# An attention and SwiGLU kernel: the halves of the attention weights on ScalarE and GpSimd, a plan entry for them, and a third factor from hi and u

## The chip, the cores and the metric

One core of one Trainium2 chip. The metric is the device time of one execution in microseconds (us); executions of one kernel agree within about 0.2%, so differences of 1 to 2 us are near the limit of what medians tell, and smaller ones are read from traces.

## The reference, cut to what matters

```python
def mab(q, kv):                       # attention with scale 1/sqrt(C)
    s = scale * (q @ kv.transpose(0, 2, 1))
    a = np.exp(s - s.max(-1, keepdims=True)); a /= a.sum(-1, keepdims=True) + 1e-09
    return a @ kv
h = mab(I, x)                         # 4 batches, 12416 tokens, 32 inducing points, C = 128
x2 = mab(x, h)
xn = x2 / rms(x2) * rms_g             # SwiGLU feed-forward, hidden width 1536
out = (silu(xn @ w_gate) * (xn @ w_val)) @ w_out
```

The kernel folds h into the gate and value weights, so that the feed-forward reads the attention weights themselves (32 per token) and not x2.

## The kernel before

The tokens go through in 100 units of mostly 512; each unit has 12 steps, one for 128 hidden channels: 1200 steps. A step is a gate matmul, silu on ScalarE, an output product of an older step, a value matmul, and u = silu x value on VectorE.

```python
ps_gv = pool("ps_gv", 4, space=PSUM)          # banks of gate and value
...
for j in range(NJ):
    g = ps_gv.tile(...);  nc.tensor.matmul(g[:, 0:T], sg[:, ts(j, P)], a[:, 0:T], start=True, stop=True)
    nc.scalar.activation(sl[:, 0:T], g[:, 0:T], AF.Silu)
    products(j)                               # output products of older steps
    v = ps_gv.tile(...);  nc.tensor.matmul(v[:, 0:T], sv[:, ts(j, P)], a[:, 0:T], start=True, stop=True)
    nc.vector.tensor_tensor(out=t[:, 0:T], in0=sl[:, 0:T], in1=v[:, 0:T], op=ALU.mult)
    steps(j)                                  # pieces of attention work, splits among them
    if (b, u, j) in ready:
        soon(1, lambda j=j, t=t: three(j, t)) # u as three factors, one step later
    else:
        plain.append(lambda j=j, t=t: project(wo[:, j, :], t[:, 0:T]))
```

A plain output product is a full fp32 matmul. In some steps u is written as hi + lo, and three single-pass matmuls, with hi, lo and a third factor d, take its place. ScalarE makes hi and a scaled hi (hs), GpSimd makes lo and d:

```python
def three(j, t):
    ...
    nc.scalar.activation(hi, v, AF.Copy, scale=1.0 - 2.0 ** -13)
    nc.gpsimd.tensor_tensor(out=lo, in0=v, in1=hi.bitcast(F32), op=ALU.subtract)
    def rest():                               # one step later
        nc.scalar.activation(hs[:, 0:T], hi.bitcast(F32), AF.Copy, scale=2.0 ** -12)
        nc.gpsimd.tensor_tensor(out=d, in0=hs[:, 0:T], in1=lo.bitcast(F32), op=ALU.subtract)
```

Every four units the attention weights of the next four are turned and split into halves of their own, also called hi and lo. This is the "split" of the text; 28 of them, nearly all at step 9 of a unit:

```python
def split():
    nc.vector.transpose(out=aT[rows, 0:w], in_=sc[b][rows, cols2[s]])
    nc.vector.tensor_copy(out=hi[rows, 0:w], in_=aT[rows, 0:w])
    nc.vector.tensor_tensor(out=lo[rows, 0:w], in0=aT[rows, 0:w], in1=hi[rows, 0:w].bitcast(F32), op=ALU.subtract)
```

Which steps get three factors is planned when the program is built. seam_busy says for how many us a piece of attention work keeps ScalarE and GpSimd busy; a step whose three factors would come too late by this count stays plain.

## Time and profile before

| | before |
|---|---|
| time, median of 4 (range) | 1717.5 us (1717.0 to 1718.2) |
| TensorE / VectorE / ScalarE / GpSimd busy | 98 / 69 / 71 / 69% |
| three-factor products of 1200 | 401 |
| lo of the split on VectorE, 28 of them: shortest / median / longest | 0.41 / 1.60 / 1.67 us |

### The profile page before, as it was taken

To read this page: it belongs to the slowest core of one execution; us is meant where nothing else is said; L and a number is where in the kernel's file an instruction comes from. 1 tells how busy PE (TensorE), PEld (TensorE's weight loads), DVE (VectorE), ACT (ScalarE), POOL (GpSimd) and SP (SyncE) were. 2 spreads that over 40 slices of the span, in tenths; PEclk is the share of its full clock that TensorE was granted. 3 is DMA by queue.
4 is the path that set the end of the run, shared out by engine and by line. 5 is a ranking of instruction groups with operands and counts; after the bars stand their busy time and mean duration, and the time that the engine had idled before them with its cause. 6 is when DMAs were issued, how large, how long until landed. Compare 5 with 4: busy or idle time off the path is not lost. (4 is left out here: it accounts for less than half of the span.)

```text
span 1715.7 us, 23430 instructions
## 1 busy us (share of the span) xinstructions
PE 1675.3 (98%) x6855; PEld 1046.2 (61%) x6855; DVE 1189.4 (69%) x1982; ACT 1222.4 (71%) x2180; POOL 1181.4 (69%) x936
## 2 busy tenths in 40 slices
PE   9899999999999999999999999999999999999998
PEld 7545565655566656665556656566556666666666
DVE  4867876777668776667667877667767666666665
ACT  4346777676777777776777777767677887788786
POOL 0317775776487776676657877577657888888875
PEclk9999999999999999999999999999999999999999
DMA  6344433433343232434334314153211121112111
GB/s 248 87 68 74 81 69 78 103 80 64 62 79 63 47 71 41 105 76 91 67 59 83 58 34 83 36 129 77 50 30 35 32 38 31 35 34 37 31 36 24
DMA packets 389359, 112.65 MB, mean 66 GB/s; under 512 B 365136, under 2 KB 369776, under 8 KB 386672
## 3 DMA queue, kind: packets, MB, share of 16 engines
q1 hardware_dynamic: 388944, 111.02, 32.3%
q8 instruction: 54, 0.88, 0.2%
q14 instruction: 73, 0.60, 0.1%
q10 hardware_dynamic: 288, 0.15, 0.0%
HBM read 53.95 MB, written 27.00 MB: 47 GB/s over the span
## 5 line engine op out<-in xcount | busy, mean ns | idle before, releaser
L607 DVE TENSOR_TENSOR u<-silu,gv 128x512 f32<-128x512 f32 (+2 forms) x1200 | 788.2, 665 | 471.9 <-PE gv L605 276.6
L602 ACT ACTIVATE silu<-gv 128x512 f32<-128x512 f32 (+2 forms) x1200 | 698.6, 584 | 414.7 <-PE gv L600 377.2
L550 PE MATMUL acc<-u,wo 128*128 128x512 f32 (+2 forms) x1598 | 793.9, 581 | 7.0 <-DVE u L607 5.8
L605 PE MATMUL gv<-a,sv 128*128 128x512 f32 (+2 forms) x1200 | 768.1, 640 | 1.3 <-ACT silu L602 0.7
L588 POOL TENSOR_TENSOR xn<-u,xn 128x512 fp32r<-128x512 f32 (+2 forms) x401 | 507.8, 1266 | 314.7 <-ACT xn L587 250.0
L593 POOL TENSOR_TENSOR xn<-hs,xn 128x512 fp32r<-128x512 f32 (+2 forms) x401 | 507.0, 1264 | 53.4 <-POOL xn L588 16.7
L600 PE MATMUL gv<-a,sg 128*128 128x512 f32 (+2 forms) x1200 | 492.5, 410 | 14.3 <-ACT silu L602 6.5
L600 PEld LDWEIGHTS gv<-a,sg 128*128 128x128 f32 x1200 | 227.6, 190 | 255.3 <-ACT silu L602 117.1
L550 PEld LDWEIGHTS acc<-u,wo 128*128 128x128 f32 x1598 | 299.1, 189 | 87.5 <-issue 17.9
L605 PEld LDWEIGHTS gv<-a,sv 128*128 128x128 f32 x1200 | 227.7, 190 | 196.5 <-issue 142.3
L587 ACT ACTIVATE xn<-u 128x512 fp32r<-128x512 f32 (+2 forms) x401 | 248.1, 619 | 18.8 <-DVE u L607 18.1
L592 ACT ACTIVATE hs<-xn 128x512 f32<-128x512 f32 (+2 forms) x401 | 246.3, 614 | 8.8 <-POOL xn L593 8.2
L550 PE MATMUL acc<-xn,xn 128*128 128x512 f32 (+2 forms) x401 | 159.0, 396 | 6.2 <-POOL xn L593 5.9
L568 PE MATMUL u<-xn,xn 128*128 128x512 f32 (+2 forms) x401 | 155.8, 388 | 0.0
L566 PE MATMUL u<-xn,xn 128*128 128x512 f32 (+2 forms) x401 | 155.4, 388 | 0.0
L492 POOL TENSOR_TENSOR rs<-ms,mhalf 128x16 f32<-128x16 f32 (+2 forms) x28 | 75.5, 2698 | 43.0 <-DVE ms L490 42.9
L550 PEld LDWEIGHTS acc<-xn,xn 128*128 128x128 f32 x401 | 75.3, 188 | 29.9 <-POOL xn L593 14.1
L568 PEld LDWEIGHTS u<-xn,xn 128*128 128x128 f32 x401 | 75.4, 188 | 17.1
L566 PEld LDWEIGHTS u<-xn,xn 128*128 128x128 f32 x401 | 75.3, 188 | 15.6
L559 DVE STREAM_TRANSPOSE o<-o 128x512 f32<-128x512 f32 (+2 forms) x97 | 67.7, 698 | 3.4
L558 DVE TENSOR_TENSOR o<-acc,o 128x512 f32<-128x512 f32 (+2 forms) x97 | 64.9, 669 | 0.0
L571 ACT ACTIVATE o<-u 128x512 f32<-128x512 f32 (+2 forms) x97 | 56.4, 582 | 0.2
(155 smaller groups left out, 746.2 us busy)
## 6 DMA issues: line engine op xcount, KB each, us to landing
out_dram<-o SPq DMA_DIRECT2D x320, 64.0 KB, 2.0
xT<-in_x_dram SPq DMA_DIRECT2D x60, 256.0 KB, 4.6
xn<-in_x_dram SPq DMA_DIRECT2D x60, 256.0 KB, 4.4
a<-hi SPq DMA_DIRECT2D x160, 64.0 KB, 2.0
a<-lo SPq DMA_DIRECT2D x158, 64.0 KB, 2.0
w<-w SPq DMA_DIRECT2D x22, 256.0 KB, 3.2
xn<-in_x_dram SPq DMA_DIRECT2D x5, 1024.0 KB, 10.8
out_dram<-o SPq DMA_DIRECT2D x64, 60.0 KB, 2.0
```

What stands on the lines that cost most here:

```text
L492: nc.gpsimd.tensor_tensor(out=rs, in0=ms, in1=mhalf[rows, 0:n], op=ALU.pow)
L550: nc.tensor.matmul(acc[:, 0:T], lhsT, rhs, start=st["left"] == NJ, stop=st["left"] == 1)
L566: nc.tensor.matmul(ups[:, 0:T], w[:, i, :], hi, start=st["k"] == nk, stop=False)
L568: nc.tensor.matmul(ups[:, 0:T], w[:, NK + i, :], lo, start=False, stop=not st["k"])
L587: nc.scalar.activation(hi, v, AF.Copy, scale=1.0 - 2.0 ** -13)
L588: nc.gpsimd.tensor_tensor(out=lo, in0=v, in1=hi.bitcast(F32), op=ALU.subtract)
L592: nc.scalar.activation(hs[:, 0:T], hi.bitcast(F32), AF.Copy, scale=2.0 ** -12)
L593: nc.gpsimd.tensor_tensor(out=d, in0=hs[:, 0:T], in1=lo.bitcast(F32), op=ALU.subtract)
L600: nc.tensor.matmul(g[:, 0:T], sg[:, ts(j, P)], a[:, 0:T], start=True, stop=True)
L602: nc.scalar.activation(sl[:, 0:T], g[:, 0:T], AF.Silu)
L605: nc.tensor.matmul(v[:, 0:T], sv[:, ts(j, P)], a[:, 0:T], start=True, stop=True)
L607: nc.vector.tensor_tensor(out=t[:, 0:T], in0=sl[:, 0:T], in1=v[:, 0:T], op=ALU.mult)
```

## The change

Its intent is to free VectorE at the splits, by giving hi to ScalarE and lo to GpSimd, to tell the plan so, and to make d without lo: hi(1 + 2^-12) - u is the same number as hi x 2^-12 - (u - hi).

```diff
-            nc.vector.tensor_copy(out=hi[rows, 0:w], in_=aT[rows, 0:w])
-            nc.vector.tensor_tensor(out=lo[rows, 0:w], in0=aT[rows, 0:w], in1=hi[rows, 0:w].bitcast(F32), op=ALU.subtract)
+            if b or s:
+                nc.scalar.copy(out=hi[rows, 0:w], in_=aT[rows, 0:w])
+            else:
+                nc.vector.tensor_copy(out=hi[rows, 0:w], in_=aT[rows, 0:w])
+            engine.tensor_tensor(out=lo[rows, 0:w], in0=aT[rows, 0:w], in1=hi[rows, 0:w].bitcast(F32), op=ALU.subtract)
 ...
-                nc.scalar.activation(hs[:, 0:T], hi.bitcast(F32), AF.Copy, scale=2.0 ** -12)
-                nc.gpsimd.tensor_tensor(out=d, in0=hs[:, 0:T], in1=lo.bitcast(F32), op=ALU.subtract)
+                nc.scalar.activation(hs[:, 0:T], hi.bitcast(F32), AF.Copy, scale=1.0 + 2.0 ** -12)
+                nc.gpsimd.tensor_tensor(out=d, in0=hs[:, 0:T], in1=v, op=ALU.subtract)
 ...
-                seam_busy[at] = seam_busy.get(at, 0) + {2: 1.4, 3: 3.0, 4: 1.2}.get(i, 0)
+                seam_busy[at] = seam_busy.get(at, 0) + {2: 1.4, 3: 3.0, 4: 1.2, 5: 1.4}.get(i, 0)
```

(engine is GpSimd except at the first split.) So the change has three parts: the *move* of hi and lo, the *plan* entry, and the *third* factor.

## The prediction

> **What bounds the kernel now.** I read the page first (busy shares, slices, chain of waits), then the groups with shapes kept apart, the waits, and the timeline of single stretches.
>
> ```profile
> PE 1675.3 (98%) x6855; PEld 1046.2 (61%) x6855; DVE 1189.4 (69%) x1982; ACT 1222.4 (71%) x2180; POOL 1181.4 (69%) x936
> ...
> PE   9899999999999999999999999999999999999998
> ...
> PEclk9999999999999999999999999999999999999999
> ...
> PE 22%; issue 0%; DVE 0%; ACT 0%; POOL 0%; DVEq 0%; POOLq 0%
> ```
>
> TensorE is busy in every slice at full clock, and the three engines that the change touches idle 30% each. The chain of waits agrees: its largest named parts are TensorE's (PE 22%, all others 0%). So the change counts only in two ways: by passes added to TensorE, and by moments at which TensorE waits for another engine.
>
> A steady stretch of TensorE's timeline (start in us, duration, engine, line, tiles) gives the price of a step, one of the 1200 blocks of 128 hidden channels:
>
> ```profile
> 806.17 0.40 PE L600 MATMUL gv<-a,sg 128*128 128x512 f32 x1
> 806.40 1.02 PE L550 MATMUL acc<-u,wo 128*128 128x512 f32 x2
> 806.86 0.80 PE L605 MATMUL gv<-a,sv 128*128 128x512 f32 x1
> 807.49 0.40 PE L600 MATMUL gv<-a,sg 128*128 128x512 f32 x1
> ```
>
> Gate to gate, a step with a plain fp32 output product takes 807.49 - 806.17 = 1.32 us (1.325 over several). In a step with the three-factor product (hi, lo, and the third factor d) the gates stand at 1370.30 and 1371.46: 1.16 us. A three-factor product is worth 1.325 - 1.16 = 0.165 us; 401 of 1200 are made so.
>
> One split, where VectorE turns the attention weights (aT), rounds them to hi and subtracts for lo, looks like this:
>
> ```profile
> 1370.59 0.69 DVE L607 TENSOR_TENSOR u<-silu,gv 128x512 f32<-128x512 f32 x1 [0.67 <-ACT hs L592]
> 1371.20 0.70 DVE L500 STREAM_TRANSPOSE aT<-sc 128x512 f32<-128x512 f32 x1
> 1371.94 0.50 DVE L502 CAST hi<-aT 128x512 fp32r<-128x512 f32 x1
> 1372.48 1.66 DVE L503 TENSOR_TENSOR lo<-aT,hi 128x512 fp32r<-128x512 f32 x1
> 1374.06 1.87 DVE L607 TENSOR_TENSOR u<-silu,gv 128x512 f32<-128x512 f32 x3
> ```
>
> ScalarE and then TensorE in the same stretch:
>
> ```profile
> 1370.73 0.60 ACT L602 ACTIVATE silu<-gv 128x512 f32<-128x512 f32 x1 [0.21 <-PE gv L600]
> ...
> 1371.89 0.60 ACT L602 ACTIVATE silu<-gv 128x512 f32<-128x512 f32 x1
> ```
>
> ```profile
> 1372.79 0.39 PE L600 MATMUL gv<-a,sg 128*128 128x512 f32 x1
> ...
> 1373.71 0.40 PE L605 MATMUL gv<-a,sv 128*128 128x512 f32 x1
> 1374.79 0.51 PE L600 MATMUL gv<-a,sg 128*128 128x512 f32 x1 [0.68 <-DVE u L607]
> ```
>
> VectorE spends 1374.06 - 1371.94 = 2.1 us on hi and lo. The next u is late, its PSUM bank is not free, and the gate matmul starts 1.08 us after the value matmul where 0.23 is regular: 0.85 us lost. I went through all 28 splits so. Twelve lose 0.6 to 1.14 us, 10.9 together, and all twelve wait for u; three (near 264, 678 and 1091 us) lose 0.83 each, about half of it waiting for silu; the one near 135 us loses 4.4, of which 2.86 wait for GpSimd's d; the rest lose nothing.
>
> **What the Trainium skill says.** "FP8 and Floating Point Precision", TensorE Precision Notes: a true fp32 product takes four passes through the array. The trace agrees: 1.325 less two single-pass matmuls of 0.23 leaves 0.865. "GPSIMD Engine Reference", 4.1 Engine selection, calls GpSimd about twice as slow on two inputs; here 1.29 us against VectorE's 0.69. "VectorE: DVE Perf Modes", TRN2 errata, gives ScalarE 224 + FD cycles at 1.2 GHz, for 512 elements 613 ns; hs (128x512) shows 626. The same page, in "Two Vector instructions with no wait between them", says that VectorE's second SBUF read is shared with GpSimd. The trace fits that: lo takes 1.66 us here with GpSimd running, and 0.69 at 264.49 and 135.42, where GpSimd is idle.
>
> **The change part by part.**
>
> *Fewer three-factor products.* The new entry 5: 1.4 tells the plan that ScalarE and GpSimd are busy at a split, so it plans fewer. The order of instructions of the changed kernel has 383 in place of 401: 14 of 512 columns and 4 of 480 fewer. Evaluating the plan shows 17 of the 18 are the block at which a split itself falls (step 9 of a unit), one lies just after the first late split. Cost on TensorE, the bound: 18 x 0.165 = +2.9 us.
>
> *VectorE loses hi and lo at 27 of 28 splits* (the first stays): 27 x about 0.5 and 0.4 to 1.67, some 45 us, all on an engine that idles 30%. Only the waits count: the 10.9 us above.
>
> *ScalarE gets hi, 27 x about 0.62 = 16 us,* and loses 18 x 2 x 0.62 = 22 (0.62 is the row of hs, a copy of the same size; that hi costs the same is my estimate). The total is nothing; the place is what matters. In its queue hi stands after silu of this step and before silu of the next, and it waits for aT, which VectorE begins only after this step's u. In the split shown: aT ends 1371.90, hi runs 1371.96 to 1372.58, and the silu that began at 1370.73 begins 1.85 us later and ends 1373.18. The gate matmul two steps on, at 1372.79 before, takes that silu's bank: it starts at about 1373.28, a loss of 0.5. The next u follows that silu at once, is done by 1373.9, and the later gate that waited for it before no longer does. So 0.85 becomes about 0.5. Repeating this at every split, with its own times of aT, silu and gate: the twelve keep 6.2 of 10.9 (gain 4.7). Near 264, 678 and 1091 I get about 1.06 in place of 0.83 (+0.7). Three splits that lost nothing (near 408, 822, 1235) get 0.44 each (+1.3), and the three narrow ones (32x256) 0.23 each (+0.7). The five where TensorE has transforms of the next batch to do in between stay at 0. Sum: -4.7 + 2.7 = -2.0 us.
>
> *GpSimd gets lo,* 27 x about 1.2 = 33 us, and loses 18 x 2.53 = 46. It stands where a three-factor pair was taken out, and the transfers that gather hi and lo have 10 steps, about 13 us, before the matmul that reads them, against 2 us of landing. I count 0.
>
> *d from hi scaled up, minus u.* In both forms lo and d run in order on GpSimd, with the same durations, and TensorE needs both. What goes is a wait of GpSimd for its own lo: 16.7 us over 30 times in the waits view, on an engine off the path. Where TensorE waits for d (0.63 and 0.78 near 388 and 420, again in the next two batches), the timeline has another GpSimd instruction, the product z or a subtraction of maxima, in front of d. That stays. u is held a little longer, but it has eight buffers. About -0.5 us.
>
> *The start near 135 us.* d there waits behind the 2.9 us power rs, so the 2.86 stay; with VectorE free afterwards, perhaps -1 us.
>
> Sum: +2.9 - 2.0 - 0.5 - 1.0 = -0.6; 1717.8 - 0.6 = 1717.2, so 1717.
>
> **The rivals.** *The wait simply goes:* if silu is not held up by hi (a later place in the queue, or enough slack in the banks), all 10.9 us of the twelve go and none of the new 2.7 comes: 1717.8 + 2.9 - 10.9 - 1.5 = about 1708. For it: ScalarE idles 29%. Against: the queue is in order and hi stands directly before silu. *The wait moves to ScalarE and grows:* if each late silu makes not one but two gates wait, about 0.5 more at 20 splits, 1727. For it: in steady state silu begins within 0.05 us of its gate, and only two steps of banks lie between. Against: after the late silu ScalarE catches up with 0.7 us of idle per plain step. *GpSimd becomes the bound:* 69% busy with bursts; lo put into a burst would delay d and TensorE would wait for d more often. But 13 us less work in all, and the plan keeps room: I give it at most 3 us. *Buffers:* the build chooses PSUM banks anew; in the changed program a gate waits for the silu just before it 32 times, not 51. This can give or take 1 to 2 us anywhere.
>
> **Range and chances.** The parts are small and of both signs; the least sure is the new wait at ScalarE (0 to twice what I put) and the choice of banks. So 1711 to 1723 for 8 in 10. 2% is 34 us, over three times all split losses together: within 2% has 0.98.
>
> **What would show it right or wrong.** Right: 383 products of three factors and TensorE's passes up by 18; VectorE's share down by about 3 points; at the splits the gates' waits for u gone or small, and a wait of about 0.5 for silu in their place; silu starting some 1.8 us late just after each hi. Wrong if silu's delay costs TensorE nothing (1708), if waits for d grow, or if the lost products do not cost 0.165 each because those steps were waiting anyway.

## The result, and the profile after

The changed kernel took 1712.85 us (median of 4, 1711.66 to 1714.15) against 1717.51. The ratio is 0.9973, interval 0.9955 to 0.9990. (A ratio here is the mean time of one kernel's fast runs over that of the other's in the same rounds, so not quite the ratio of the medians.) By the 2% rule it is the same; but it is 4.7 us faster where I had said 0.5, and inside the range by 1.9 us.

The page of the changed kernel, busy times and chain of waits:

```profile
PE 1677.0 (98%) x6837; PEld 1042.5 (61%) x6837; DVE 1145.1 (67%) x1928; ACT 1220.4 (71%) x2171; POOL 1153.0 (67%) x927
...
PE 88%; ACT 4%; DVE 3%; issue 2%; POOL 2%; SPq 1%; DMA 0%; ACTq 0%; DVEq 0%; POOLq 0%
```

TensorE still sets the end. It has 18 instructions fewer: 18 three-factor products (3 instructions) became plain ones (2). It is busy 1.7 us longer here, but its repetition e0_after (below) shows 1675.0, so the busy time does not carry the price of the lost products; the starts of the gates below do. VectorE lost 44 us, and that alone is no gain.

The same split as in the prediction, now about 2 us earlier; first VectorE, then ScalarE, TensorE, GpSimd (line numbers are up to 4 higher than before):

```profile
1368.56 0.69 DVE L611 TENSOR_TENSOR u<-silu,gv 128x512 f32<-128x512 f32 x1 [0.64 <-ACT hs L596]
1369.16 0.70 DVE L501 STREAM_TRANSPOSE aT<-sc 128x512 f32<-128x512 f32 x1
1371.11 1.29 DVE L611 TENSOR_TENSOR u<-silu,gv 128x512 f32<-128x512 f32 x2 [1.24 <-ACT silu L606]
```

```profile
1369.90 0.62 ACT L504 CAST hi<-aT 128x512 fp32r<-128x512 f32 x1 [1.39 <-DVE aT L501]
1370.43 1.78 ACT L606 ACTIVATE silu<-gv 128x512 f32<-128x512 f32 x3
```

```profile
1370.14 0.80 PE L609 MATMUL gv<-a,sv 128*128 128x512 f32 x1
1371.07 0.50 PE L604 MATMUL gv<-a,sg 128*128 128x512 f32 x1
```

```profile
1368.65 1.29 POOL L597 TENSOR_TENSOR xn<-hs,u 128x512 fp32r<-128x512 f32 x1
1370.60 1.29 POOL L507 TENSOR_TENSOR lo<-aT,hi 128x512 fp32r<-128x512 f32 x1 [0.66 <-ACT hi L504]
```

ScalarE stands idle 1.39 us until aT is there; its queue holds two silus whose gates began at 1368.29 and 1369.45, but hi is ahead of them. VectorE then idles 1.24 us for silu, and the gate at 1371.07 is 0.29 us late. This is the wait that the prediction named, at about half the size. VectorE's 2.1 us for hi and lo, and the 0.85 they cost TensorE, are gone.

To see where the 4.5 us between the two traces come from, the start of each of the 1200 gate matmuls of one trace is set against the other:

| what | predicted, us | found in the traces, us |
|---|---|---|
| 18 lost products | +2.9 | +2.7 for 17 (0.14 to 0.16 each, some steps after the split); the 18th lies in the start |
| twelve splits, waits 10.9 before | 6.2 after: -4.7 | 3.3 after: -7.6 |
| three splits near 264, 678, 1091 | +0.7 | +1.1 |
| three near 408, 822, 1235 | +1.3 | +1.1 |
| three narrow ones | +0.7 | 0 |
| small waits near 480 to 510 us, in three batches | part of -0.5 for d | -2.6 |
| two of the five splits with transforms, near 546 and 959 | 0 | -0.4 |
| start, up to 150 us | -1.0 | +1.0 |
| after the last gate | 0 | +0.2 |
| sum | -0.6 | -4.5 |

So far the story would be: right mechanism, sizes off. The experiments show that the story was not right.

### The profile page after: what moved, and what is told of

Read it like the earlier page. It is cut to its first block, busy times and chain, and to the rows that moved or that the text cites. A ratio compares the mean times of both kernels' runs of the same rounds, so it can differ in the third digit from the quotient of the medians.

```text
span 1711.2 us, 23282 instructions
## 1 busy us (share of the span) xinstructions
PE 1677.0 (98%) x6837; PEld 1042.5 (61%) x6837; DVE 1145.1 (67%) x1928; ACT 1220.4 (71%) x2171; POOL 1153.0 (67%) x927
## 4 chain that ended last, share of the span: by engine, by line
PE 88%; ACT 4%; DVE 3%; issue 2%; POOL 2%; SPq 1%; DMA 0%; ACTq 0%; DVEq 0%; POOLq 0%
PE acc L554 40%; PE gv L604 16%; PE gv L609 14%; PE u L572 5%; PE u L570 5%; PE mm L302 2%; DVE u L611 1%; PE mm L479 1%; PE acc L179 1%; ACT silu L606 1%; PE mm L359 1%; DVE aT L501 1%; PE gv L293 1%; ACT hi L504 1%; ACT hs L596 1%
## 5 line engine op out<-in xcount | busy, mean ns | idle before, releaser
L554 PE MATMUL acc<-u,wo 128*128 128x512 f32 (+2 forms) x1634 | 811.5, 581 | 4.3 <-DVE u L611 3.1
L592 POOL TENSOR_TENSOR xn<-u,xn 128x512 fp32r<-128x512 f32 (+2 forms) x383 | 482.0, 1258 | 357.1 <-ACT xn L591 268.7
L604 PE MATMUL gv<-a,sg 128*128 128x512 f32 (+2 forms) x1200 | 493.0, 411 | 11.8 <-ACT silu L606 8.7
L597 POOL TENSOR_TENSOR xn<-hs,u 128x512 fp32r<-128x512 f32 (+2 forms) x383 | 482.5, 1260 | 23.5 <-ACT hs L596 22.1
L554 PEld LDWEIGHTS acc<-u,wo 128*128 128x128 f32 x1634 | 305.3, 189 | 86.2 <-issue 18.0
L591 ACT ACTIVATE xn<-u 128x512 fp32r<-128x512 f32 (+2 forms) x383 | 236.9, 618 | 14.7 <-DVE u L611 13.1
L596 ACT ACTIVATE hs<-xn 128x512 f32<-128x512 f32 (+2 forms) x383 | 235.0, 614 | 4.4 <-POOL xn L597 3.3
L554 PE MATMUL acc<-xn,xn 128*128 128x512 f32 (+2 forms) x383 | 150.4, 393 | 6.0 <-POOL xn L597 6.0
L572 PE MATMUL u<-xn,xn 128*128 128x512 f32 (+2 forms) x383 | 148.4, 388 | 0.0
L570 PE MATMUL u<-xn,xn 128*128 128x512 f32 (+2 forms) x383 | 148.2, 387 | 0.0
L572 PEld LDWEIGHTS u<-xn,xn 128*128 128x128 f32 x383 | 71.9, 188 | 16.3
L570 PEld LDWEIGHTS u<-xn,xn 128*128 128x128 f32 x383 | 71.9, 188 | 14.4
## 6 DMA issues: line engine op xcount, KB each, us to landing
xn<-in_x_dram SPq DMA_DIRECT2D x5, 1024.0 KB, 10.9
```

The costliest lines, as they stand in the source:

```text
L554: nc.tensor.matmul(acc[:, 0:T], lhsT, rhs, start=st["left"] == NJ, stop=st["left"] == 1)
L570: nc.tensor.matmul(ups[:, 0:T], w[:, i, :], hi, start=st["k"] == nk, stop=False)
L572: nc.tensor.matmul(ups[:, 0:T], w[:, NK + i, :], lo, start=False, stop=not st["k"])
L597: nc.gpsimd.tensor_tensor(out=d, in0=hs[:, 0:T], in1=v, op=ALU.subtract)
```

## The experiments

All gave correct results. Every call ran the kernel before on the same chip; its median was 1717.8, 1717.8 and 1718.1 us. I write the difference to it. Three theories were to be told apart: A, the gain is at the splits, where long waits for u become shorter waits for silu; B, the relief of VectorE makes it; C, the third factor d comes earlier.

### One part at a time

Four kernels: third factor only (e1_third), plan entry only (e2_plan), move only (e3_move), and the change without the third factor (e4_no_third). The edits are the three pieces of the diff above, for e2_plan just this line on the kernel before:

```diff
-  {2: 1.4, 3: 3.0, 4: 1.2}
+  {2: 1.4, 3: 3.0, 4: 1.2, 5: 1.4}
```

> Only the third factor is made the new way (hi scaled up, minus u); halves and plan as before, 401 three-factor products. Theory A (the gain is at the splits: waits for u of 0.85 to 1.13 us become waits for silu of 0.3 to 0.4): nothing at the splits, so -0.1 to -0.8 us against before, from two small waits for d near 501 and 510 us (about 0.12 each, in each of three batches). Theory C (the gain is d coming earlier): -3 us or more, and the waits for d near 482 and 500 us gone.

> Only the plan's entry for the split is added: 383 three-factor products in place of 401, halves still on VectorE. Theory A: 18 x 0.16 = +2.9 us for the lost products; the waits for u at the twelve splits stay at 0.85 to 1.13; if the loss of 0.47 us per batch boundary that the trace of the change shows before the split near 487 us comes from the plan (it takes the products there one step later) and not from d, -1.4, together +1.5 us; otherwise +2.9. Theory B (VectorE's load decides): +2.9, the same. Theory C: +2.9.

> Only the halves move to ScalarE and GpSimd; plan and third factor as before, 401 products. Theory A: the twelve splits go from 10.9 to about 3.4 us of waiting, three near 264, 678, 1091 us lose 0.26 each more, three near 408, 822, 1235 us 0.22 each more: -6 us, if GpSimd and ScalarE can take the halves beside the products of the same steps; if they can't, waits for d at the 17 splits give back up to 17 x 0.3 = 5 us. Theory B: -6 or better. Theory C: 0.

> The changed kernel with the old third factor (halves moved, plan entry kept, 383 products). Theory A: -4.5 + 0.1 to 0.8, so -3.7 to -4.4 us against before. Theory C: the gain is gone, 0 to +1 us. Theory B: as A.

| kernel | parts | time, us (range) | to before |
|---|---|---|---|
| e1_third | third | 1714.3 (1714.1 to 1715.1) | -3.5 |
| e2_plan | plan | 1709.2 (1707.2 to 1709.6) | -8.6 |
| e3_move | move | 1711.7 (1711.1 to 1713.8) | -6.0 |
| e4_no_third | move + plan | 1713.9 (1713.8 to 1715.4) | -3.9 |
| the change | move + plan + third | 1712.9 (1711.7 to 1714.2) | -4.7 |

Move and e4_no_third came as theory A had them. Two did not. The third factor alone gave 3.5 us. Its trace shows many small pieces and none of 3: the splits lose 0.74 where they lost 0.85, and near 480 to 510 us, at each of three batch boundaries, 0.6 to 0.7 go (between 478 and 512 us TensorE's weight loads wait 1.5 us for d before, 0.6 now). So theory C holds for a part of this gain; A had at most 0.8. And the plan entry alone, for which every theory had +1.5 to +2.9, is the fastest of these five: it gains nearly twice what the whole change gains, while nothing moves from VectorE. Gate by gate, the waits of the twelve splits go entirely (-10.9), small waits just before the splits near 490, 903 and 1316 us go too (-1.4), and two of the five others give -0.4; the lost products cost +2.8, and +1.7 at the start are most likely chance of the clock (see the end of this part); together -8.2 between these two traces.

The split of e2_plan, VectorE and GpSimd:

```profile
1367.52 0.70 DVE L500 STREAM_TRANSPOSE aT<-sc 128x512 f32<-128x512 f32 x1
1368.26 0.51 DVE L502 CAST hi<-aT 128x512 fp32r<-128x512 f32 x1
1368.81 0.69 DVE L503 TENSOR_TENSOR lo<-aT,hi 128x512 fp32r<-128x512 f32 x1
1369.42 1.88 DVE L607 TENSOR_TENSOR u<-silu,gv 128x512 f32<-128x512 f32 x3
```

```profile
1365.84 1.29 POOL L588 TENSOR_TENSOR xn<-u,xn 128x512 fp32r<-128x512 f32 x1
1367.20 1.29 POOL L593 TENSOR_TENSOR xn<-hs,xn 128x512 fp32r<-128x512 f32 x1
```

lo takes 0.69 us, not 1.66, and GpSimd has ended at 1368.49, before lo begins. In the kernel before, GpSimd was at work through nearly all of lo (1372.48 to 1374.14), and was itself slower than its usual 1.29:

```profile
1372.12 1.47 POOL L588 TENSOR_TENSOR xn<-u,xn 128x512 fp32r<-128x512 f32 x1
1373.66 1.61 POOL L593 TENSOR_TENSOR xn<-hs,xn 128x512 fp32r<-128x512 f32 x1
```

These two are the subtractions for the three-factor product of step 9, the very step of the split, and that product is what the plan entry takes away at 17 splits. The longest lo over all 28 splits tells it too (the row gives shortest, median and longest in ns), the kernel before first:

```profile
L503 DVE TENSOR_TENSOR lo<-aT,hi x28: 411/1602/1668, 57.0 to 1682.4; 128x512 fp32r<-128x512 f32 x20, 128x480 fp32r<-128x480 f32 x4, 32x256 fp32r<-32x256 f32 x4
```

```profile
L503 DVE TENSOR_TENSOR lo<-aT,hi x28: 411/692/695, 57.6 to 1674.7; 128x512 fp32r<-128x512 f32 x20, 128x480 fp32r<-128x480 f32 x4, 32x256 fp32r<-32x256 f32 x4
```

From this came theory A2: the costly thing was not hi and lo on VectorE, but lo beside GpSimd's work. The plan entry cures that. The move cures it as well, by another way, and then the entry only costs: with the move, adding it made 1711.7 into 1713.9.

### Is it GpSimd's work that slows lo?

The lost product relieves ScalarE too (hi and hs), so GpSimd's part had to be shown by itself. e10_idle is e2_plan with useless work for GpSimd just after aT at four splits of the last batch, two-input subtractions at two of them, one-input copies at the others. Its output is 256 columns wide; e12_wide repeats it 512 wide, with hs as the place to write.

```diff
+            if b == 3 and 1 <= s <= 4:
+                idle = third.tile([P, 512], F32, name="hs")          # e10_idle: [P, 256], 4 times
+                for _ in range(2 if s <= 2 else 3):
+                    if s <= 2: nc.gpsimd.tensor_tensor(out=idle[:], in0=aT[:], in1=aT[:], op=ALU.subtract)
+                    else:      nc.gpsimd.tensor_copy(out=idle[:], in_=aT[:])
```

> The plan-only kernel with useless work for GpSimd right after aT at four splits of the last batch: at two of them four two-input subtractions of 128x256, at the next two four one-input copies of 128x256. Theory A2: at the first two lo on VectorE takes 1.3 to 1.7 us instead of 0.69, and TensorE waits 0.5 to 0.9 us for u there, +1 to +1.8 us in all. If any work on GpSimd does it, the copies do the same and it is +2 to +3.6; if only two-input work, the copies leave lo at 0.69. Rival (the lost product relieves ScalarE, not GpSimd): lo stays 0.69 at all four, 0 us.

> As e10_idle, but the useless GpSimd work is 512 wide, as the product's own subtractions are: two two-input subtractions at two splits of the last batch, three one-input copies at the next two. Theory A2 (two-input work of GpSimd slows lo, and long instructions more than short ones, against 0.98 us beside 256-wide ones): lo 1.5 to 1.7 us at the first two, TensorE waits 0.6 to 0.9 there; beside the copies lo at most 0.8 and no wait. Rival (the width does not matter and most of the earlier slowdown had another cause, such as ScalarE's work): lo about 0.98 again.

e12_wide, one split of each kind, GpSimd and then VectorE:

```profile
1367.38 2.55 POOL L505 TENSOR_TENSOR hs<-aT 128x512 f32<-128x512 f32 x2
...
1492.27 2.39 POOL L507 COPY hs<-aT 128x512 f32<-128x512 f32 x3
```

```profile
1367.62 1.41 DVE L510 TENSOR_TENSOR lo<-aT,hi 128x512 fp32r<-128x512 f32 x1
...
1492.53 0.98 DVE L510 TENSOR_TENSOR lo<-aT,hi 128x512 fp32r<-128x512 f32 x1
```

The first of each GpSimd group alone, the one under way when lo begins:

```profile
1367.38 1.10 POOL L505 TENSOR_TENSOR hs<-aT 128x512 f32<-128x512 f32 x1
...
1492.27 0.69 POOL L507 COPY hs<-aT 128x512 f32<-128x512 f32 x1
```

| GpSimd beside lo | of its instruction, left when lo begins, us | lo, us | TensorE's wait at that split, us |
|---|---|---|---|
| nothing | 0 | 0.69 | 0 |
| copies, 256 wide | 0.22 | 0.77 | 0 |
| copies, 512 wide | 0.43 to 0.45 | 0.98 to 1.00 | 0.16 to 0.20 |
| subtractions, 256 wide | 0.43 | 0.98 | 0.17 to 0.19 |
| subtractions, 512 wide | 0.87 | 1.41 | 0.61 |
| a product's own subtractions (kernel before) | 1.11 | 1.66 | 0.85 |

So GpSimd's work alone brings the slow lo and TensorE's wait back, with ScalarE as in e2_plan (busy 1207.9 us in all, against 1207.8): the rival falls. Both expectations missed in part. At 256 wide lo rose to 0.98 and not to 1.3, and one-input copies slow it too, which I had put at no more than 0.8 in the wide case. The second column tells why, and the expectations did not have it: in every row below the first, lo ends 0.54 to 0.55 us after the end of the GpSimd instruction that was under way when it began. So does every slow lo of 128x512 in the kernel before and in e1_third, 30 in all. In these runs neither the kind nor the width of GpSimd's work counts by itself, but how much of that one instruction is left; 512-wide copies and 256-wide subtractions both leave 0.43 and both give 0.98. By the traces lo waits for that instruction to end, and does not share with it. TensorE's wait follows lo: it is about what lo takes beyond 0.8 us. The times carry nothing here: 1708.6 (e10_idle) and 1710.4 us (e12_wide) lie on both sides of the 1709.2 that e2_plan took. It was run at another time.

### What does the move cost?

e5_hi_dve leaves lo on GpSimd and gives hi back to VectorE. e9_plan_third has no move at all. e7_late keeps hi on ScalarE but puts hi and lo one step later in the queues, about when aT is ready:

```diff
-            if b or s: nc.scalar.copy(out=hi[rows, 0:w], in_=aT[rows, 0:w])
-            ...                                   # lo as in the change
+            def make():
+                if b or s: nc.scalar.copy(out=hi[rows, 0:w], in_=aT[rows, 0:w])
+                ...                               # lo as in the change
+            if (b, s) in ((0, 0), (0, 1)): make()
+            else: soon(1, make)
```

> The changed kernel with hi made by VectorE again; lo stays on GpSimd. Theory A2 (formed on the plan-only run: lo on VectorE was slow because GpSimd was running the two-input subtractions of the split step's own product; the plan entry takes that product away; and hi on ScalarE holds silu up): silu no longer waits for hi, so the 0.2 to 0.4 us at fifteen splits and part of the 0.9 at three are gone, -4 to -6 us against the changed kernel, 1707 to 1709. Theory B (relieving VectorE makes the gain): slower than the changed kernel or the same, 1713.

> The changed kernel without the move: plan entry and new third factor, halves on VectorE. Theory A2: the gains of the plan entry (-8.2) and part of the third factor's (-1.3, as between the changed kernel with and without it) add up: 1707 to 1709, 4 to 6 us faster than the changed kernel, so the move to ScalarE and GpSimd costs time. Theory B: about +3 us slower than the changed kernel, 1716.

> The changed kernel, but hi and lo are put one step later in the queues of ScalarE and GpSimd, when aT is ready. Theory A2: silu waits for hi by at most 0.6 us where ScalarE has that slack, the waits of 0.28 to 0.38 at the splits go to 0: -4 to -6 us against the changed kernel, 1707 to 1709. Theory B: nothing changes for VectorE, so the same as the changed kernel, 1713.

| kernel | time, us (range) | to before |
|---|---|---|
| e5_hi_dve | 1706.1 (1705.7 to 1707.0) | -11.8 |
| e9_plan_third | 1705.7 (1705.4 to 1707.1) | -12.1 |
| e7_late | 1704.6 (1703.8 to 1706.6) | -13.2 |
| the change again (e0_after) | 1712.4 (1711.7 to 1712.6) | -5.8 |

> The changed kernel once more, on the chip of the two others, so that they can be set against it: 1712 to 1714 us. If it lies outside, the differences between runs of different calls are not to be trusted to 1 us.

The repetition e0_after came as expected. All three beat the change by 6 us or more, a little better than expected, and theory B (the gain is VectorE's relief) is out: e9_plan_third has VectorE at 69% as before and is as good as e5_hi_dve. Against the changed kernel, each of the three gains 0.29 at the splits of the last batch, 0.39 near 490, 903 and 1316 us, 0.22 near 408, 822 and 1235 us, and 0.64 near 264, 678 and 1091 us: the waits for silu, one for one, and at all but the last three about 0.1 more in the step after (e5_hi_dve and e9_plan_third give 0.3 of each 0.64 back soon after). ScalarE of e7_late at the same split shows why one step is enough:

```profile
1361.73 0.60 ACT L612 ACTIVATE silu<-gv 128x512 f32<-128x512 f32 x1 [0.21 <-PE gv L610]
1362.91 0.62 ACT L505 CAST hi<-aT 128x512 fp32r<-128x512 f32 x1 [0.58 <-DVE aT L501]
1363.43 0.59 ACT L612 ACTIVATE silu<-gv 128x512 f32<-128x512 f32 x1
```

The silu that had stood behind hi now runs before it. hi still waits 0.58 us for aT, but in front of work that is only just ready: the next silu is at most 0.6 us late, and no gate waits (the next one starts at 1363.78, 0.63 us after its value matmul, the regular distance behind a plain product).

### Is the plan entry needed when nothing waits?

e8_late_full is e7_late without the entry: 401 three-factor products again.

> As e7_late (hi and lo one step later on ScalarE and GpSimd), but without the plan's entry for the split: 401 three-factor products. Theory A2: the entry pays where it frees GpSimd during a lo on VectorE; here no lo is on VectorE, so only its cost is left, and the 18 products are worth 18 x 0.16 = 2.9 us: 1702, 3 us faster than e7_late. Rival: GpSimd cannot take lo beside that step's own product, d comes late and TensorE waits for d at up to 17 splits by 0.2 or more: 1705 or slower.

It took 1703.7 us (1703.0 to 1704.4), 14.5 below the kernel before, and is the fastest. The expected 3 us against e7_late did not show in the medians (1.3 when each is set against its own kernel before). The traces say why. At most splits e8_late_full does gain 0.14 to 0.17, the price of one product, and no wait for d takes it back there; but it loses 0.2 to 0.4 net at each of the three batch boundaries (the first near 490 us) and 0.35 once near 676, and at the start it lost 1.4 us that have another cause. Two windows from 128 to 148 us, the changed kernel and then its repetition e0_after (the last figures are granted clock, DMA share and GB/s):

```profile
128.00:148.00 20.00, 16.55 (x48) 9.42 (x47) 13.02 (x20) 11.01 (x22) 13.01 (x10) 0.91 0.38 63
```

```profile
128.00:148.00 20.00, 16.57 (x53) 9.64 (x52) 14.40 (x23) 12.46 (x24) 14.30 (x11) 1.00 0.34 58
```

One and the same kernel gets 0.91 of the clock there in one execution and all of it in another; e7_late had 1.00 and e8_late_full 0.91. Between these two executions the gates of this stretch shift by 1.7 us. So the first 150 us can carry that much chance, and whether e8_late_full beats e7_late is left open.

## Why the prediction was right or wrong

The range held. The sum of -0.6 came out as -4.7, and one step of the reasoning was wrong in kind. That the range held all the same is partly luck: inside the change the move takes away the same waits that the plan entry takes away by itself, so crediting the wrong part did not show in the sum. The chain of waits that was read as agreeing (PE 22%, all others 0%) covers only 22% of the span; the chain of the changed kernel, which is followed throughout, has ScalarE and VectorE with 4 and 3%.

*Fewer three-factor products: "Cost on TensorE, the bound: +2.9."* The price was right, 0.16 each in the traces. The step failed in taking this for the whole effect of the entry. By itself it gains 8.6 us, because 17 of the 18 lost products are those whose GpSimd work slowed lo; at the twelve splits that is worth 10.9 us, and small waits elsewhere go with it, another 1.8, whose cause was not followed up. The prediction had every part of that on the table (the read shared with GpSimd, lo at 0.69 where GpSimd idles, the lost product at the step of the split) and did not put them together.

*"Only the waits count: the 10.9 us above", credited to VectorE losing hi and lo.* Wrong as a cause: e9_plan_third keeps hi and lo on VectorE and has no such waits at the splits of the last batch. What made u late was the slow lo. Within the change the move does remove the waits, but it is not needed for that.

*ScalarE's hi.* Mechanism right, size off. From aT's end to the late gate I put 0.06 + 0.62 + 0.60 + 0.10 = 1.38 us. Measured: 1369.86 to 1371.07, 1.21. About half of the difference of 0.17 is hi's 0.62: the next silu starts 0.53 after hi starts, while hi is still shown running. The rest is the way from the start of that silu to the gate, 0.64 and not 0.70, and from aT to hi, 0.04 and not 0.06. So twelve splits keep 3.3 and not 6.2. It is still a loss: the hi of e5_hi_dve, on VectorE, costs nothing.

*GpSimd's lo: 0.* Right; no wait for d appeared at the splits.

*d: -0.5.* Too small alone (-3.5 on the kernel before), nearer in the change (-1.0 between e4_no_third and the change; 0.4 to 0.7 at each of three batch boundaries by the traces). The pieces it counts in are of 0.1 us, which I had dropped as off the path.

*The start: -1.0.* It was +1.0, most likely by chance of the clock: between 60 and 86 us it was 0.87 of full in the trace before and 0.80 after.

*The rivals.* "The wait simply goes", about 1708, is what e7_late made of it, with the change's other parts: 1704.6. "The wait moves to ScalarE and grows" and "GpSimd becomes the bound" did not come.

## What to carry to other kernels

Before moving an instruction off an engine, ask why it is slow where it stands: if the same form takes 0.69 us in one place and 1.66 in another, look at what the other engines do in those very microseconds. An entry in a planning table is a change like any other and wants a run of its own. And an instruction that must wait for its operand should not stand in an in-order queue ahead of work that is ready; here one step later was worth 7 to 8 us.

## What the Trainium skill lacked or had wrong

Nothing that these runs show. Two points look like gaps beside the passages that the prediction names, but other pages of the Trainium skill have them, and the runs agree:

- What sharing the second SBUF read costs is in "SBUF — State Buffer", Summary: rules for kernel authors: a VectorE instruction with two SBUF inputs and a GpSimd instruction that reads SBUF do not share, and the one that starts second waits until the first is done. Here lo (0.69 us alone) ends 0.54 to 0.55 us after the end of the GpSimd instruction that it found under way, 0.77 to 1.67 us in all, and a product's second subtraction on GpSimd, begun while lo ran, took 1.61 in place of 1.29.
- ScalarE's 613 ns for 512 elements are a duration (hi showed 617 to 620), not what the queue loses. "ScalarE: Activation LUTs", What ACT_TABLE_LOAD costs, says that neighbouring ACTIVATEs overlap by about 93 ns; here the silu behind hi, a copy, started 0.53 us after hi did.
